# A recurrent attention feeding a mixture of experts: a sum of rows cut into pieces, and two groups of transfers moved to later iterations

## The chip, the core and the metric

The kernel runs on one core of a Trainium2 chip. Its engines work side by side and meet at semaphores: TensorE (PE), VectorE (DVE), ScalarE (ACT), GpSimd (POOL) and SyncE (SP). SP only issues transfers here. Each engine takes its instructions in the order in which they were written, so an instruction that waits holds up everything behind it on that engine. The metric is the device time of one execution in microseconds (us); lower is better.

## What is computed

First a recurrent attention over 4 batches, 8 heads, 768 steps and head width 48, in float32, then a mixture of 8 experts on the 3072 rows that come out of it:

```python
for t in range(S):                                   # attention
    cur = np.einsum('bhd,bhe->bhde', u[None] * kt, vt)
    y[:, :, t] = np.einsum('bhd,bhde->bhe', rt, state + cur)
    state = wt[:, :, :, None] * state + np.einsum('bhd,bhe->bhde', kt, vt)

logits = x @ w_gate + modality_bias[modality_id]     # x: the 3072 rows of 384
e_idx = np.argmax(logits, axis=1)
probs = np.exp(logits - logits.max(-1, keepdims=True))
probs /= probs.sum(-1, keepdims=True) + 1e-09
gate_w = probs[np.arange(N), e_idx]
for e in range(E):                                   # 384 -> 1024 -> 384
    mask = e_idx == e
    h = np.maximum(x[mask] @ w1[e], 0.0)
    out[mask] = gate_w[mask, None] * (h @ w2[e])
```

## The kernel before

**The attention.** The 768 steps of a batch are cut into 6 chunks of 128, so there are 24 units of 128 rows, numbered over all batches. A software pipeline of 26 iterations (`for i in range(-2, NU)`, L970) calls `att_iter(i)`, which works on three units at once: `a = i + 2`, `m = i + 1` and `z = i`. In one iteration

- DVE makes for unit `a` a scan of decays backwards (L413), the scaled keys K (L343, called at L417), a reciprocal and a copy W (L418, L419), a scan forwards and the scaled rows R (`rows_op`, L371), and for unit `m` the masked product A (L462). Between the first scan and the keys it adds two parts of the output of unit `z - 1`, `pY` from TensorE and `dV` from ACT and POOL, into its row buffer `xb` (`x_rows`, L540, calling `x_add`, L537). For units 10 to 13 (`far`) ACT and POOL do that sum.
- POOL makes products for unit `a + 1`: the decays `pw` (L307), `G` (L311) and, in place, the inputs of the next keys and rows (L324). Without these DVE's scan, keys and rows of the next iteration can't start.
- TensorE makes transposes of keys and of sums, the scores `pS` (L460), the state update `pU` (L483), the output `pY` (L503, L514) and the logits (L568). `pS` and `pY` have one buffer each: the next is written when DVE has read the last.

**What SP issues, in order.** At the end of iteration `i`: one of four stores that clear 512 dummy rows of the DRAM buffer `xs` (`fill`, iterations 2 to 5), one of sixteen 192 KB pieces of the first expert's weights (`w_raw` into `raw`, iterations 6 to 21), three loads of r, k and w for unit `i + 6` (until iteration 17) and one load of v for unit `i + 3`. `behind` makes a transfer wait for an instruction of DVE in that iteration: fills and weights for the first scan, v for the masked product.

**The scatters.** The first units are sorted by expert early: in iterations 15 to 20 (`DRAIN`) POOL ends each iteration with one indirect store that scatters 128 finished rows into `xs` (`scatter`, L771). The scatters among themselves write different rows, which `rows_apart` declares, so none waits for another. The fills are declared nothing: a fill and a scatter are two stores into the same DRAM buffer, and the framework orders them as they were written.

**The handover.** After the scatter of iteration 20, `blk_load(0)` (L794; `LOAD = 20`) reads the first block of 512 rows back from `xs` into `xq`. DVE transposes it (L819), ACT and DVE split it into two parts `xh` and `xo` (L827, L829), and TensorE starts the first expert (`blk_up`, L843). From there on 7 blocks are worked off by TensorE, with weights split in two by ACT, DVE and POOL (`w_split`).

Of the kernel before, what the change touches and what calls it, by code (L numbers as in the profile page):

```python
# [14 lines left out]
ALU = mybir.AluOpType  # L15
# [3 lines left out]
P = 128  # L19
NCH = S // P  # L20
NU = B * NCH
NT = B * S
DM = H * D
E, F = 8, 1024
KC = DM // P
FC = F // P
# [4 lines left out]
BW = 512  # L31
# [36 lines left out]
SCATTER = PART[0] + 3  # L68
NEAR = 6
DRAIN = {SCATTER + 2 + n: 1 for n in range(NEAR)}  # L70
EARLY = 6
FILL = 2
APART = 1
NPW = 3
LOAD = SCATTER + 1 + NEAR


@with_exitstack
def kernel(ctx: ExitStack, tc: tile.TileContext, rkw, vt, wf, cst, mid, wg, bias, w1, w2, out):
    nc = tc.nc  # L80
# [20 lines left out]
    ins = [pa.tile([P, WO + WIN], F32, name=f"in{i}", bufs=1) for i in range(NIN)]  # L101
    pw = [pa.tile([P, 4 * SEG], F32, name=f"pw{i}", bufs=1) for i in range(NPW)]
    KT = wk.tile([P, 2, 4, 64], F32, name="KT", bufs=1)
    T = {}

    def wt(n, tag, sh, bufs=None, dt=F32):
        T[tag, n] = (pa if tag in PREP else wk if tag in WORK else rt).tile(sh, dt, tag=tag, name=f"{tag}{n}", bufs=bufs)
        return T[tag, n]
# [7 lines left out]
    def behind(dma, key):  # L116

        if key in step:
            tc.add_manual_dep(dma.ins, step[key].ins.name, mybir.DependencyInfo(mybir.DependencyClass.Sync, mybir.DependencyReason.DATA),
                              reason="transfers of an iteration issued apart")  # L120
# [6 lines left out]
    def r_of(n):  # L127
        return ins[n % NIN][:, RO:RO + 512]
# [4 lines left out]
    def w_of(n):  # L133
        return ins[n % NIN][:, WO:WO + WIN].rearrange("p (a c b) -> p a c b", a=4, c=2)[:, :, :, 0:P // 2]
# [120 lines left out]
    def fill(j):  # L255
        return nc.sync.dma_start(out=xs[DUMMY + j * P:DUMMY + j * P + P, :], in_=zt)
# [36 lines left out]
    def w_raw(e, k, part, cond=None, parts=2):  # L293
        n = FC // parts
        kw = {} if cond is None else {"cond": cond}
        return nc.sync.dma_start(out=raw[k][:, part * n:part * n + n, :].rearrange("p f c -> p (f c)"),
                                 in_=(w1, w2)[k][ds(e, 1), :, part * n * DM:(part + 1) * n * DM].rearrange("a p c -> (a p) c"), **kw)
# [7 lines left out]
    def decays(n, eng):  # L305
        w = w_of(n)
        eng.tensor_tensor(out=heads(pw[n % NPW])[:, :, 2:SEG - 1], in0=w[:, :, 0], in1=w[:, :, 1], op=ALU.mult)  # L307

# [22 lines left out]
    def spread(n, tag, src, c0, bufs=None):  # L331
        X = sides(wt(n, tag, [P, 4, P], bufs).rearrange("p a b -> p (a b)"))
        be, k, v = heads(BE)[:, :, c0:c0 + P // 2], 1 if tag == "K" else 0, sides(src)
        if n == 0:
            w = sides((r_of, k_of)[k](NIN - 1))
            nc.vector.tensor_tensor(out=X[:, :, k], in0=v[:, :, k], in1=be, op=ALU.mult)
            nc.vector.tensor_tensor(out=X[:, :, 1 - k], in0=w[:, :, 1 - k], in1=be, op=ALU.mult)
        elif on_vec(n, k):
            nc.vector.tensor_tensor(out=X[:, :, k], in0=v[:, :, k], in1=be, op=ALU.mult)
            nc.vector.tensor_tensor(out=be, in0=be, in1=w_of(n)[:, :, k], op=ALU.mult)  # L340
            nc.vector.tensor_tensor(out=X[:, :, 1 - k], in0=v[:, :, 1 - k], in1=be, op=ALU.mult)
        else:
            nc.vector.tensor_tensor(out=X, in0=v, in1=be[:, :, None, :].to_broadcast([P, 4, 2, P // 2]), op=ALU.mult)  # L343

    def first(n):
        return n % NCH == 0

    def ok(n):
        return 0 <= n < NU
# [18 lines left out]
    def scan(pp, way):  # L368
        return nc.vector.tensor_tensor_scan(out=BE[:, ::way], data0=pp[:, ::way], data1=d1[:, ::way], initial=0.0, op0=ALU.mult, op1=ALU.max)  # L369

    def rows_op(a):  # L371
        step["second", a - 2] = scan(pw[a % NPW], 1)
        spread(a, "R", r_of(a), 1, 3)

    def dV_tile(z):
# [9 lines left out]
    def att_iter(i):  # L385
        a, m, z = i + 2, i + 1, i
# [11 lines left out]
        if ok(z):  # L398
            if z < NU - 1:
                dV_tile(z)  # L400
            dV, v0, dT = dV_parts(z)
# [6 lines left out]
        if ok(a):  # L408
            t, W = ins[a % NIN], wt(a, "W", [P, 4], 2)
            if a == 0:  # L410
                decays(a, nc.vector)
            pp, n = pw[a % NPW], 4 * SEG
            step["first", i] = scan(pp, -1)  # L413
        if ok(z - 1) and not far(z - 1):
            x_rows(z - 1)
        if ok(a):
            spread(a, "K", k_of(a), 3)  # L417
            nc.vector.reciprocal(out=pp[:, 1:n:SEG], in_=BE[:, 2:n:SEG])  # L418
            nc.vector.tensor_copy(out=W, in_=BE[:, 2:n:SEG])  # L419
        if i == NU - 1:  # L420
            blk_turn(0, (2,))
        if ok(a) and i != -1:
# [54 lines left out]
        if ok(m) and not last:  # L477
# [3 lines left out]
            for h in range(H):  # L481
                p, hh = divmod(h, 2)
# [27 lines left out]
        if ok(z):  # L510
            for h in range(H):
                p, hh = divmod(h, 2)
# [21 lines left out]
    def far(n):  # L534
        return PART[0] <= n <= SCATTER

    def x_add(n, eng, y):  # L537
        eng.tensor_tensor(out=T["xb", n][:, 0:DM], in0=y, in1=T["dV", n].rearrange("p a b -> p (a b)"), op=ALU.add)

    def x_rows(n, eng=None):  # L540
        c = int(n >= PART[0])
        if n in FROM:
            T["xp", c] = (xa, rt)[c].tile([P, PART[c], XW], F32, tag="xp", name=f"xp{c}", bufs=1)
        T["xb", n] = T["xp", c][:, n - FROM[c]]
        y = T["pY", n][:, 0:DM]
        if eng is None:
            x_add(n, nc.vector, y)
        else:
            eng.copy(out=T["xb", n][:, 0:DM], in_=y)

# [417 lines left out]
        pend.extend(range(FROM[c], FROM[c] + PART[c]))  # L968

    for i in range(-2, NU):  # L970
        if EARLY <= i < EARLY + 2 * FC:
            if i == EARLY:
                e0 = nc.sync.value_load(e0i[0:1, 0:1], min_val=0, max_val=E - 1)
        if 1 <= i < 1 + len(SETUP):
            hooks.append(SETUP[i - 1])
        if i == PART[0] + 1:
            ra, tb = route_a(0), table(0)
            hooks.extend([lambda: next(ra), lambda: [*ra], lambda: hook_b(0), lambda: [*tb]])
        if i == NU - 1:
            prep.close()  # L980
        att_iter(i)
        if FILL <= i < FILL + BW // P:
            behind(fill(i - FILL), ("first", i))
        if EARLY <= i < EARLY + 2 * FC:
            behind(w_raw(e0, (i - EARLY) // FC, (i - EARLY + 2) % FC, parts=FC), ("first", i))
        apart = i >= APART
        if i >= -1 and ok(i + 3) and not apart:
            loadv(i + 3)
        if i == -2:
            load(3)  # L990
        if i == 0:
            early()
        if ok(i + 2 + NIN):
            load(i + 2 + NIN, ((512, 1024),))
            load(i + 2 + NIN, ((1024, LIN),), ("second", i) if apart else None)
        if ok(i + 2 + NIN):
            load(i + 2 + NIN, ((0, 512),))
        if ok(i + 3) and apart:
            loadv(i + 3, ("mask", i))
        drain(DRAIN.get(i, 0))  # L1000
        if i == LOAD:
            blk_load(0)
# [28 lines left out]

    part = lambda fn, *a, **k: (lambda: fn(*a, **k))
    q0, q1 = seq[0:2]
    x_rows(NU - 1)
    at(q0, "u", 1, lambda: x_cols(NU - 2, pt(("x", 0), "pX")), lambda: x_cols(NU - 1, pt(("x", 1), "pU")))
    at(q0, "u", 3, part(logits, NU - 2), part(logits, NU - 1))
    for g in range(FC):
# [264 lines left out]
```

## Time and profile before

| what | value |
|---|---|
| median of 3 runs | 331.17 us (330.54 to 331.27) |
| profiled execution, own time | 331.58 us |
| its span, first to last instruction | 329.7 us |
| PE busy | 321.0 us, 97% |
| DVE busy | 237.4 us, 72% |
| ACT busy | 206.3 us, 63% |
| POOL busy | 149.6 us, 45% |
| granted TensorE clock, mean | 0.997 |

All rows below are from the profiled execution. Busy shares are means over the span and hide two stages: the attention up to about 119 us, and the blocks of the experts after it. A PE that shows busy may still run behind another engine, since its matmuls are pipelined and their ends are modelled; starts of instructions say more than busy shares.

### The profile page before, as it was taken

What the parts mean: (1) busy time and instruction counts of PE and PEld (TensorE: products, weight loads), DVE (VectorE), ACT (ScalarE), POOL (GpSimd) and SP (SyncE); (2) the same over time, 40 slices, a digit from 0 to 9 for tenths busy, and PEclk for the clock granted to TensorE, in tenths of its full rate; (3) what the DMA queues carried; (4) which work ended last, traced back from release to release, by engine and by line L of the source; (5) the groups of instructions that cost most, each with busy time, mean ns of one, the idle gap of its engine ahead of it and who ended that gap; (6) DMA issues with size and microseconds to landing.
All of it is one profiled execution on the core that took longest, in us unless ns stands there. A gap on an engine that the chain in (4) does not pass through costs nothing. (4 is left out here: it accounts for less than half of the span.)

```text
span 329.7 us, 10271 instructions
## 1 busy us (share of the span) xinstructions
PE 321.0 (97%) x3917; PEld 297.5 (90%) x3917; DVE 237.4 (72%) x509; ACT 206.3 (63%) x516; POOL 149.6 (45%) x196
## 2 busy tenths in 40 slices
PE   8999999999999999999999999999999999999993
PEld 3789899999998988899889999999999988999983
DVE  7999999999999875795559758858358445815520
ACT  1687587688889894471459456956956944614420
POOL 6889998889886088145861210210210220121022
PEclk9999999999999999999999999999999999999998
DMA  7988988888895601615954800540550673310011
GB/s 260 401 285 254 287 268 268 259 265 261 278 294 163 146 7 55 138 73 188 306 180 123 256 32 2 119 168 2 121 190 4 167 174 97 95 73 22 0 34 55
DMA packets 39023, 52.50 MB, mean 159 GB/s; under 512 B 19221, under 2 KB 26165, under 8 KB 38964
## 3 DMA queue, kind: packets, MB, share of 16 engines
q1 hardware_dynamic: 35860, 42.28, 43.7%
q0 software_dynamic: 3104, 9.47, 7.7%
q8 instruction: 33, 0.54, 0.7%
q14 instruction: 26, 0.21, 0.3%
HBM read 55.63 MB, written 11.88 MB: 205 GB/s over the span
## 5 line engine op out<-in xcount | busy, mean ns | idle before, releaser
L886 POOL DMA_INDIRECT out<-ot,xg x24 | 26.3, 1095 | 128.4 <-ACT ot L885 126.3
L848 DVE SCALAR_TENSOR_TENSOR hl<-pS_u,hh 128x512 fp32r<-128x512 f32 (+2 forms) x56 | 34.6, 618 | 60.7 <-ACT hh L847 60.6
L843 PE MATMUL pS_u<-xh,wh 128*128 128x512 f32 (+2 forms) x168 | 61.1, 364 | 0.0
L843 PE MATMUL pS_u<-xh,wl 128*128 128x512 f32 (+2 forms) x168 | 60.8, 362 | 0.0
L847 ACT ACTIVATE hh<-pS_u 128x512 fp32r<-128x512 f32 (+2 forms) x56 | 30.3, 541 | 48.5 <-PE pS_u L843 48.5
L302 DVE TENSOR_TENSOR wl<-raw,wh 128x768 fp32r<-128x768 f32 x52 | 48.8, 962 | 2.3 <-ACT wh L301 2.0
L301 ACT CAST wh<-raw 128x768 fp32r<-128x768 f32 (+1 forms) x60 | 44.9, 786 | 0.0
L843 PE MATMUL pS_u<-xo,wh 128*128 128x512 f32 (+2 forms) x168 | 42.8, 363 | 0.0
L773 POOL DMA_INDIRECT xs<-xp,posT x24 | 26.3, 1097 | 21.3 <-DVE posT L656 18.1
L369 DVE TENSOR_TENSOR_SCAN pX_s<-pw,pX_s 128x268 f32<-128x268 f32 x48 | 34.3, 715 | 1.2 <-POOL pw L307 0.3
L864 PE MATMUL pY_d<-wh,hh 128*128 128x384 f32 x104 | 35.1, 337 | 0.0
L864 PE MATMUL pY_d<-wh,hl 128*128 128x384 f32 x104 | 35.0, 336 | 0.0
L864 PE MATMUL pY_d<-wl,hh 128*128 128x384 f32 x104 | 34.9, 336 | 0.0
L843 PEld LDWEIGHTS pS_u<-xh,wh 128*128 128x128 f32 x168 | 31.6, 188 | 3.1
L843 PEld LDWEIGHTS pS_u<-xh,wl 128*128 128x128 f32 x168 | 31.6, 188 | 2.8
L843 PEld LDWEIGHTS pS_u<-xo,wh 128*128 128x128 f32 x168 | 30.9, 188 | 3.3 <-DVE xo L829 0.3
L390 ACT ACTIVATE dV<-v,dT 128x48 f32<-128x48 f32 x120 | 29.7, 328 | 0.2 <-POOL pw L307 0.2
L462 DVE TENSOR_TENSOR A<-pS,cs 128x1024 f32<-128x1024 f32 x24 | 29.2, 1218 | 0.6 <-PE pS L460 0.6
L311 POOL TENSOR_TENSOR G<-in 128x512 f32<-128x512 f32 x24 | 26.1, 1090 | 3.6 <-PE pR_x L355 2.5
L460 PE MATMUL pS<-R,K 64*128 64x128 f32 x384 | 27.3, 281 | 0.0
L864 PE MATMUL pX_d<-wh,hh 128*128 128x384 f32 x80 | 27.0, 337 | 0.0
L864 PE MATMUL pX_d<-wh,hl 128*128 128x384 f32 x80 | 26.9, 336 | 0.0
(331 smaller groups left out, 676.1 us busy)
## 6 DMA issues: line engine op xcount, KB each, us to landing
raw<-w SPq DMA_DIRECT2D x24, 768.0 KB
in<-rkw SPq DMA_DIRECT2D x46, 256.0 KB
in<-rkw SPq DMA_DIRECT2D x22, 264.0 KB
v<-vt SPq DMA_DIRECT2D x24, 192.0 KB
wg<-wf SPq DMA_DIRECT2D x8, 576.0 KB
raw<-w SPq DMA_DIRECT2D x16, 192.0 KB
xs<-zt SPq DMA_DIRECT2D x12, 193.0 KB
xq<-xs SPq DMA_DIRECT2D x12, 192.0 KB
```

Source lines behind the costliest of these rows:

```text
L301: nc.scalar.copy(out=wh[k][:, sl], in_=raw[k][:, sl])
L302: (eng or (nc.vector, nc.gpsimd)[k]).tensor_tensor(out=wl[k][:, sl], in0=raw[k][:, sl], in1=wh[k][:, sl].bitcast(F32), op=ALU.subtract)
L369: return nc.vector.tensor_tensor_scan(out=BE[:, ::way], data0=pp[:, ::way], data1=d1[:, ::way], initial=0.0, op0=ALU.mult, op1=ALU.max)
L390: nc.scalar.activation(out=dV[:, h], in_=v0[:, h], func=AF.Copy, scale=dT[:, h:h + 1])
L460: nc.tensor.matmul(out=pS[:, hh, p], lhsT=K[q, p], rhs=R[q, p], start=True, stop=True)
L462: step["mask", i] = nc.vector.tensor_tensor(out=a2(A), in0=a2(pS), in1=mask[:, None, :].to_broadcast([P, H, P]), op=ALU.mult)
L773: rows_apart("xs", nc.gpsimd.indirect_dma_start(out=xs[:, :], out_offset=bass.IndirectOffsetOnAxis(ap=posT[:, n:n + 1], axis=0), in_=T["xb ...
L843: nc.tensor.matmul(out=pp, lhsT=wsrc[0][:, g, c * P:(c + 1) * P], rhs=xsrc[:, c, 0:w], start=(n == 0), stop=(n == 3 * KC - 1))
L847: nc.scalar.activation(out=hh, in_=pp, func=AF.Relu)
L848: nc.vector.scalar_tensor_tensor(out=hl, in0=pp, scalar=0.0, in1=hh.bitcast(F32), op0=ALU.max, op1=ALU.subtract)
L864: nc.tensor.matmul(out=X["y", q, j][0:r1 - r0], lhsT=hsrc[:, r0:r1], rhs=wsrc[1][:, f], start=(f == 0 and n == 0), stop=(f == FC - 1 and n ...
L886: ins = nc.gpsimd.indirect_dma_start(out=out[:, :], out_offset=bass.IndirectOffsetOnAxis(ap=xg[0:m, j, 1:2].bitcast(I32), axis=0), in_=ot[ ...
```

## The change

Three edits.

1. The sum of a unit's rows on DVE is cut into three pieces of 128 columns, put after the first scan, after the copy W and after the second scan. Where unit `a` is the first of a batch there are two pieces, of 256 and 128 columns, after the first scan and after W. In the last two iterations, which have no unit `a`, the sum stays whole.
2. The four fills move from iterations 2 to 5 to iterations 18, 18, 19 and 19.
3. The sixteen pieces of weights start in iteration 10 instead of 6; from iteration 20 on there are two in each iteration, until 22.

```diff
-EARLY = 6
-FILL = 2
+EARLY = (*range(10, 20), 20, 20, 21, 21, 22, 22)
+FILL = (18, 18, 19, 19)
+XCUTS = tuple((c, c + P) for c in range(0, DM, P))
+XLAST = ((0, 2 * P), (2 * P, DM))
...
     def rows_op(a):
         step["second", a - 2] = scan(pw[a % NPW], 1)
+        x_third(2)
         spread(a, "R", r_of(a), 1, 3)
...
         if ok(z - 1) and not far(z - 1):
-            x_rows(z - 1)
+            thirds.extend(x_rows(z - 1, cuts=((XCUTS, XLAST)[first(a)] if ok(a) else ((0, DM),))))
+        x_third(0)
         if ok(a):
             spread(a, "K", k_of(a), 3)
             nc.vector.reciprocal(out=pp[:, 1:n:SEG], in_=BE[:, 2:n:SEG])
             nc.vector.tensor_copy(out=W, in_=BE[:, 2:n:SEG])
+            x_third(1)
...
+    def x_third(k):
+        if thirds:
+            x_add(*thirds.pop(0))
...
-        if FILL <= i < FILL + BW // P:
-            behind(fill(i - FILL), ("first", i))
-        if EARLY <= i < EARLY + 2 * FC:
-            behind(w_raw(e0, (i - EARLY) // FC, (i - EARLY + 2) % FC, parts=FC), ("first", i))
+        for n, at in enumerate(FILL):
+            if i == at:
+                behind(fill(n), ("first", i))
+        for n, at in enumerate(EARLY):
+            if i == at:
+                behind(w_raw(e0, n // FC, (n + 2) % FC, parts=FC), ("first", i))
```

DVE in iteration 5 before, from the first scan to the masked product. `xp` is the row buffer that `xb` points into, `pX_s` holds the scans, and what stands in brackets are the semaphores that an instruction waits for (DVE_49 is DVE's own):

```order
L369 SCALAR_TENSOR_TENSOR pX_s<-pw_93,pX_s 128x268 [waits DVE_49,Pool_49]
L538 TENSOR_TENSOR xp_389<-pY_769,dV_722 128x384 [waits PE_49,Activation_49,Pool_49]
L343 TENSOR_TENSOR K_818<-in_91,pX_s 128x512 [waits DMAHW3_49,DVE_49,Pool_49]
L418 RECIPROCAL pw_93<-pX_s 128x4
L419 COPY W_815<-pX_s 128x4
L369 SCALAR_TENSOR_TENSOR pX_s<-pw_93,pX_s 128x268 [waits DVE_49]
L343 TENSOR_TENSOR R_823<-in_91,pX_s 128x512 [waits DMAHW5_49,DVE_49]
L462 TENSOR_TENSOR A_843<-pS_844,cs 128x1024 [waits PE_49]
```

The same iteration of the change:

```order
L371 SCALAR_TENSOR_TENSOR pX_s<-pw_93,pX_s 128x268 [waits DVE_49,Pool_49]
L543 TENSOR_TENSOR xp_389<-pY_774,dV_726 128x128 [waits PE_49,Activation_49]
L345 TENSOR_TENSOR K_822<-in_91,pX_s 128x512 [waits DMAHW3_49,DVE_49,Pool_49]
L422 RECIPROCAL pw_93<-pX_s 128x4
L423 COPY W_819<-pX_s 128x4
L543 TENSOR_TENSOR xp_389<-pY_774,dV_726 128x128 [waits Activation_49]
L371 SCALAR_TENSOR_TENSOR pX_s<-pw_93,pX_s 128x268 [waits DVE_49]
L543 TENSOR_TENSOR xp_389<-pY_774,dV_726 128x128
L345 TENSOR_TENSOR R_829<-in_91,pX_s 128x512 [waits DMAHW5_49,DVE_49]
L467 TENSOR_TENSOR A_849<-pS_850,cs 128x1024 [waits PE_49]
```

Each of the three instructions that wait for DVE itself (K, the second scan, R) now has a piece of the sum ahead of it.

SP at the end of iterations 17 to 20 before. `raw` are weights, `v` a unit's values; DMAHW semaphores are those of SP's own transfers:

```order
L137 DMA v_2248<-vt 128x384 [waits DMAHW6_49,DVE_49,Activation_49]
L296 ISA
L296 DMA raw_67<-w 128x384 [waits DMAHW7_49,DVE_49]
L137 DMA v_2353<-vt 128x384 [waits DMAHW0_49,DVE_49,Activation_49]
L296 ISA
L296 DMA raw_67<-w 128x384 [waits DMAHW1_49,DVE_49]
L137 DMA v_2466<-vt 128x384 [waits DMAHW2_49,DVE_49,Activation_49]
L296 ISA
L296 DMA raw_67<-w 128x384 [waits DMAHW3_49,DVE_49]
L137 DMA v_2579<-vt 128x384 [waits DMAHW4_49,DVE_49,Activation_49]
```

SP at the end of iterations 17 to 19 of the change. `xs<-zt` is a fill, and DMASW semaphores are those of POOL's scatters:

```order
L139 DMA v_2263<-vt 128x384 [waits DMAHW6_49,DVE_49,Activation_49]
L258 DMA xs<-zt 128x386 [waits DMAHW7_49,DMASW2_49,DVE_49]
L258 DMA xs<-zt 128x386 [waits DMAHW0_49]
L298 ISA
L298 DMA raw_67<-w 128x384 [waits DMAHW1_49]
L139 DMA v_2372<-vt 128x384 [waits DMAHW2_49,DVE_49,Activation_49]
L258 DMA xs<-zt 128x386 [waits DMAHW3_49,DMASW3_49,DVE_49]
L258 DMA xs<-zt 128x386 [waits DMAHW4_49]
L298 ISA
L298 DMA raw_67<-w 128x384 [waits DMAHW5_49]
L139 DMA v_2489<-vt 128x384 [waits DMAHW6_49,DVE_49,Activation_49]
```

The first pair of fills waits for the third scatter (DMASW2, iteration 17), the second pair for the fourth (DMASW3, iteration 18).

POOL before, from the fourth scatter (iteration 18) to the sixth (iteration 20):

```order
L773 DMA xs<-xp_389,posT 29184x386
L307 TENSOR_TENSOR pw_93<-in_90 128x4x64 [waits DMAHW7_49,DVE_49]
L311 TENSOR_TENSOR G_2359<-in_90 128x512 [waits DMAHW6_49,DMAHW0_49,PE_49]
L324 TENSOR_TENSOR in_90<-in_90 128x2x4x64 [waits Pool_49]
L773 DMA xs<-xp_389,posT 29184x386
L307 TENSOR_TENSOR pw_94<-in_91 128x4x64 [waits DMAHW4_49,DVE_49]
L311 TENSOR_TENSOR G_2472<-in_91 128x512 [waits DMAHW5_49,DMAHW3_49,PE_49]
L324 TENSOR_TENSOR in_91<-in_91 128x2x4x64 [waits Pool_49]
L773 DMA xs<-xp_389,posT 29184x386
```

The same stretch of POOL in the change:

```order
L784 DMA xs<-xp_389,posT 29184x386 [waits DMAHW7_49,DMAHW0_49]
L309 TENSOR_TENSOR pw_93<-in_90 128x4x64 [waits DVE_49]
L313 TENSOR_TENSOR G_2378<-in_90 128x512 [waits DMAHW6_49,PE_49]
L326 TENSOR_TENSOR in_90<-in_90 128x2x4x64 [waits Pool_49]
L784 DMA xs<-xp_389,posT 29184x386 [waits DMAHW4_49,DMAHW3_49]
L309 TENSOR_TENSOR pw_94<-in_91 128x4x64 [waits DVE_49]
L313 TENSOR_TENSOR G_2495<-in_91 128x512 [waits DMAHW5_49,PE_49]
L326 TENSOR_TENSOR in_91<-in_91 128x2x4x64 [waits Pool_49]
L784 DMA xs<-xp_389,posT 29184x386
```

The fourth scatter now waits for the first pair of fills (DMAHW7, DMAHW0) and the fifth for the second pair (DMAHW4, DMAHW3); the sixth waits for none, but stands behind the products of unit 23, which stand behind the fifth.

## Rows read from the trace of the kernel before

**Rows 1.** Windows: busy us per engine, clock, DMA share; attention, then blocks.

```profile
20.00:110.00 90.00, 88.01 (x2272) 83.30 (x2267) 87.49 (x170) 72.42 (x266) 75.51 (x108) 1.00 0.82 256
120.00:320.00 200.00, 200.00 (x1119) 188.68 (x1118) 124.65 (x287) 114.91 (x193) 51.66 (x48) 1.00 0.37 108
```

**Rows 2.** Timeline of DVE (start, us, instruction), iterations 12 and 16.

```profile
67.23 0.71 DVE L369 TENSOR_TENSOR_SCAN pX_s<-pw,pX_s 128x268 f32<-128x268 f32 x1
68.03 0.69 DVE L343 TENSOR_TENSOR K<-in,pX_s 128x512 f32<-128x512 f32 x1
...
85.94 0.71 DVE L369 TENSOR_TENSOR_SCAN pX_s<-pw,pX_s 128x268 f32<-128x268 f32 x1
86.56 0.54 DVE L538 TENSOR_TENSOR xp<-pY,dV 128x384 f32<-128x384 f32 x1
87.01 0.68 DVE L343 TENSOR_TENSOR K<-in,pX_s 128x512 f32<-128x512 f32 x1
...
87.70 0.13 DVE L419 COPY W<-pX_s 128x4 f32<-128x4 f32 x1
87.86 0.72 DVE L369 TENSOR_TENSOR_SCAN pX_s<-pw,pX_s 128x268 f32<-128x268 f32 x1
88.62 0.69 DVE L343 TENSOR_TENSOR R<-in,pX_s 128x512 f32<-128x512 f32 x1
```

**Rows 3.** Groups by line and shape, DVE, 15 to 113 us: busy, mean ns, idle before.

```profile
L538 DVE TENSOR_TENSOR xp<-pY,dV 128x384 f32<-128x384 f32 x17 | 9.3, 546 | 0.5 <-POOL pw L307 0.3
```

**Rows 4.** Timeline of DVE, iteration 6: a sum that starts late.

```profile
40.21 0.56 DVE L538 TENSOR_TENSOR xp<-pY,dV 128x384 f32<-128x384 f32 x1 [0.26 <-POOL pw L307]
```

**Rows 5.** Timeline of POOL: third scatter, then the fifth to the sixth.

```profile
90.53 1.01 POOL L773 DMA_INDIRECT xs<-xp,posT  x1 [0.15 <-issue]
...
99.29 1.01 POOL L773 DMA_INDIRECT xs<-xp,posT  x1 [0.15 <-issue]
100.33 0.65 POOL L307 TENSOR_TENSOR pw<-in 128x256 f32<-128x256 f32 x1
101.36 1.09 POOL L311 TENSOR_TENSOR G<-in 128x512 f32<-128x512 f32 x1 [0.37 <-PE pR_x L355]
102.53 1.10 POOL L324 TENSOR_TENSOR in<-in 128x512 f32<-128x512 f32 x1
103.78 1.01 POOL L773 DMA_INDIRECT xs<-xp,posT  x1 [0.15 <-DVE A L462]
```

**Rows 6.** Scatters, issue to landing: third to sixth; 126 to 132 us; all 24.

```profile
DMA to landing us min/median/max: 5.5/5.6/5.8
DMA to landing us min/median/max: 2.7/2.9/3.2
DMA to landing us min/median/max: 2.7/4.2/7.3
```

**Rows 7.** Timeline of SP's issues and DVE: the first load and its first reader.

```profile
0.71 2.29 SPq L125 DMA_DIRECT2D in<-rkw  x5
3.48 0.42 DVE L307 TENSOR_TENSOR pw<-in 128x256 f32<-128x256 f32 x1 [0.64 <-DMA in<-rkw]
```

**Rows 8.** Timelines of SP, DVE, ACT, PE: the first block's handover.

```profile
109.39 1.97 SPq L800 DMA_DIRECT2D xq<-xs  x4
116.40 0.71 DVE L819 STREAM_TRANSPOSE xt<-xq 128x512 f32<-128x512 f32 x1 [0.60 <-DMA xq<-xs]
117.82 0.62 ACT L827 CAST xh<-xt 128x512 fp32r<-128x512 f32 x1
119.41 0.50 PE L843 MATMUL pS_u<-xh,wh 128*128 128x512 f32 x1
```

**Rows 9.** Timeline of DVE, iteration 21: first scan of unit 23.

```profile
108.04 0.71 DVE L369 TENSOR_TENSOR_SCAN pX_s<-pw,pX_s 128x268 f32<-128x268 f32 x1
```

**Rows 10.** Windows at the end, columns as in rows 1: PE stops, then the clock.

```profile
324.00:326.00 2.00, 0.40 (x3) 0.08 (x1) 0.00 (x0) 0.58 (x1) 0.36 (x1) 1.00 0.05 14
326.00:328.00 2.00, 0.00 (x0) 0.00 (x0) 0.00 (x0) 0.00 (x0) 0.62 (x1) 0.88 0.26 98
```

More of the change, by code (lines that the diff above doesn't have):

```diff
@@ L535, in far, with x_add, x_rows @@
         return PART[0] <= n <= SCATTER
-    def x_add(n, eng, y):
-        eng.tensor_tensor(out=T["xb", n][:, 0:DM], in0=y, in1=T["dV", n].rearrange("p a b -> p (a b)"), op=ALU.add)
-    def x_rows(n, eng=None):
+    def x_add(n, eng, y, c0=0, c1=DM):
+        eng.tensor_tensor(out=T["xb", n][:, c0:c1], in0=y[:, c0:c1], in1=T["dV", n].rearrange("p a b -> p (a b)")[:, c0:c1], op=ALU.add)
+    thirds = []
+    def x_third(k):
+        if thirds:
+            x_add(*thirds.pop(0))
+    def x_rows(n, eng=None, cuts=((0, DM),)):
         c = int(n >= PART[0])
@@ L546, in x_rows @@
         if eng is None:
-            x_add(n, nc.vector, y)
+            return [(n, nc.vector, y, *c) for c in cuts]
         else:
@@ L970 @@
     for i in range(-2, NU):
-        if EARLY <= i < EARLY + 2 * FC:
-            if i == EARLY:
+        if i in EARLY:
+            if i == EARLY[0]:
                 e0 = nc.sync.value_load(e0i[0:1, 0:1], min_val=0, max_val=E - 1)
@@ L981 @@
         att_iter(i)
-        if FILL <= i < FILL + BW // P:
-            behind(fill(i - FILL), ("first", i))
-        if EARLY <= i < EARLY + 2 * FC:
-            behind(w_raw(e0, (i - EARLY) // FC, (i - EARLY + 2) % FC, parts=FC), ("first", i))
+        for n, at in enumerate(FILL):
[4 more added lines that the diff above has]
+                behind(w_raw(e0, n // FC, (n + 2) % FC, parts=FC), ("first", i))
         apart = i >= APART
@@ L1033 @@
     q0, q1 = seq[0:2]
-    x_rows(NU - 1)
+    x_add(*x_rows(NU - 1)[0])
     at(q0, "u", 1, lambda: x_cols(NU - 2, pt(("x", 0), "pX")), lambda: x_cols(NU - 1, pt(("x", 1), "pU")))
```

## The prediction

> **What bounds the kernel now.** I read the windows first, then DVE's timeline of the attention, then the timelines of POOL and SP around the handover to the first block. The windows [rows 1] show two stages. In the attention (20 to 110 us) DVE is busy 87.5 of 90 us and PE 88.0, so the two are close; in the blocks (120 to 320 us) PE is busy 200.0 of 200 us at a granted clock of 1.00, and nothing else is full. So a microsecond by which the first block starts later or earlier is a microsecond of the whole: after it there is no gap on PE that could swallow one.
>
> When does the first block start? PE's first L843 is at 119.41 [rows 8]. Backwards from there: SP issues the reads of the block at 109.39, DVE's transposes start at 116.40, having sat idle 0.60 us for them, so the reads take 7.0 us; the first xh is cast from 117.82 to 118.44. PE comes to it only at 119.41, when the attention's last products are done. So two chains end within 1.0 us of each other: the attention itself, and the block's reads with 119.41 - 118.44 = 1.0 us to spare. And the reads hang on the sixth scatter: it starts at 103.78 [rows 5] and lands 5.5 us later (the smallest of the third to sixth, [rows 6]), at 109.28, just ahead of 109.39.
>
> **The change part by part: the pieces.** In iteration 16 the scan starts at 85.94, the whole sum at 86.56, K at 87.01 [rows 2]: 1.07 us from scan to K. In iteration 12, where DVE has no sum, K starts 0.80 us after the scan (67.23 to 68.03). The sum of 0.54 us thus costs only 0.27 us today. The rows say why: K reads the scan and waits 0.09 us beyond its end, while the sum, which doesn't read it, starts 0.09 us before its end. A piece of 128 columns is 256 columns shorter than the sum of 546 ns [rows 3]; 128 more columns cost about 142 ns (R, with 512, takes 0.69 [rows 2]), so the piece takes about 0.27 us, and its slot, less the overlap of 0.09, is about 0.18 us.
> - First piece: starts 0.62 after the scan, frees DVE at 0.80, just when K could start anyway. K moves from 1.07 to 0.81: -0.26 us.
> - Second piece: today the second scan starts 0.16 us after W does (87.70 to 87.86), waiting for DVE's own results. With a piece between, 0.07 (W's 0.13 less the overlap) and 0.18 make 0.25: +0.09.
> - Third piece: R starts 0.76 us after the second scan (87.86 to 88.62), and will at 0.62 + 0.18 = 0.80 or a little more: +0.06.
>
> Together about -0.10 us in an iteration with three pieces. The two pieces of iterations 4, 10 and 16 give -0.13 and +0.09, so -0.04. Three pieces stand in iterations 1 to 9 but 4, in 15, and in 17 to 21: 14 of them; the sum is 14 x 0.10 + 3 x 0.04 = 1.5 us off DVE, 1.0 of it before the third scatter. Not all of that reaches the end, since PE is nearly as full: in iteration 6 the sum starts 0.26 us late [rows 4] although DVE was free, and such waits remain. I take 0.6 us up to the third scatter and 0.9 up to the end of the attention, with bounds of 0 and 1.5. PE can't write the next `pY` before the last piece is read; the third piece ends about 2.7 us into an iteration of 4.4 (from the scan of iteration 16 at 85.94 to that of iteration 21 at 108.04 [rows 2, 9] are five), and PE writes the next `pY` late in its own iteration, so I cost that at nothing; if the cover is gone, it is one or two tenths in a few iterations, within the bounds.
>
> Against this edit speaks a rule of the Trainium skill, "VectorE: DVE Perf Modes", section "Rules for kernel authors": chained instructions pay the flush of the pipeline each time, whether they wait on semaphores or not, so one should cut their number. The trace disagrees here: an instruction that waits for the scan starts 0.09 us after its end, and one that doesn't starts 0.09 us before it [rows 2]. What full payment would cost is a rival below.
>
> **Weights later.** The pieces of weights move, none is added. w1's eight pieces come in iterations 10 to 17, and are first used at the handover; w2's last four pieces are issued after the block's reads, where before there was one. They stand behind the reads on SP's queue and are wanted only when the block's first products are done, so I cost them at nothing. That early iterations have fewer transfers gains nothing that I can see: DVE's idle time before the sum, 0.5 us in 17 of them, is put down to POOL and not to a load [rows 3]. Bounds: a few tenths either way.
>
> **The fills.** This is the edit that decides. Before, all four were landed long before the first scatter. Now they lie between the scatters, and the order of stores into `xs` makes a chain: third scatter lands, first pair of fills is issued and lands, fourth scatter, lands, second pair, lands, fifth scatter. The sixth scatter waits for none, but it is behind unit 23's products on POOL, which are behind the fifth scatter. Then come the block's reads. In numbers:
> - The third scatter starts at 90.53 [rows 5] less 0.6, so 89.9, and lands 5.5 us later [rows 6]: 95.4. SP issues the first pair at 95.5.
> - A pair of fills: the trace has no landing of a fill. The nearest row is the first load, 264 KB, read 3.48 - 0.71 = 2.8 us after its issue [rows 7]; the second fill is issued 0.4 us after the first, and I add 0.2 for the loads ahead of them: 3.4 us. Bounds: a quiet scatter of as many bytes lands in 2.7 us of which 1.0 is POOL's own work, so 1.7 + 0.4 = 2.1; a slow one 5.8, so 5.2. First pair landed: 98.9.
> - Fourth scatter: I take the median of all, 4.2 [rows 6], since only one load of v and one of weights are beside it; bounds 2.7 and 5.8. Landed 103.1, second pair issued 103.2.
> - Second pair, with nothing ahead of it: 2.8 + 0.4 = 3.2. Landed 106.4.
> - Fifth scatter to sixth: 103.78 - 99.29 = 4.5 us, less 0.37 in which POOL waited for PE [rows 5]: 4.1. The sixth starts at 110.5.
> - Sixth scatter: by then little else is in flight, as at 126 to 132 us: 3.2 [rows 6]. Landed 113.7, reads issued at 113.8 instead of 109.39: 4.4 us late.
>
> The 1.0 us to spare at the handover goes first, which leaves 3.4 us. It can't be hidden behind other work: ACT's and POOL's splits of w1 stand behind the casts of xh or go on meanwhile, but PE has nothing left. On the way DVE also waits: its scan for unit 23, at 108.04 [rows 9] less 0.9, needs POOL's decays, which start 1.04 us after the fifth scatter, at 107.4, and take 0.65; its keys need the product in place, done at 110.3. That delays the attention's end by about 1 us, to near 119.6, less than the late reads.
>
> By another rule of the skill, "DMA: Bandwidth & Descriptors", section "Anatomy of one DMA — SWDGE (gpsimd) path", a transfer costs about 2.0 us, mostly the receipt of the write, plus its bytes over 436 GB/s. An estimate by that page gives a fill of 193 KB 2.5 us, both pairs 2.9, and the sum would be 0.8 us smaller; no row here shows a fill alone.
>
> Sum: 331.58 (the profiled execution; span 329.7 and 1.9 around it) + 3.4 = 335.0. That execution is 0.4 above the median of the runs, so the forecast is 334.6.
>
> **The rivals.**
> - *The chain hides.* All transfers land as quietly as at 126 to 132 us. Then 89.9 + 4.2 + 2.1 + 2.7 + 2.1 + 4.1 + 2.7 and 0.2 for issues is 108.0: the sixth scatter lands no later than today, the attention's end decides, and its 0.9 us are won: 330.3. It decides where the reads are issued by 109.39 + 1.0 less what the attention wins. For it: landings of 2.7 to 3.2 exist, and SP's queue is emptier after iteration 17. Against it: the third to sixth scatters all took 5.5 to 5.8, in this very place [rows 6].
> - *The chain is long and the clock falls.* Landings stay at 5.5, pairs take 4.0: 89.9 + 5.5 + 4.0 + 5.5 + 4.0 + 4.1 + 5.5 + 0.3 = 118.8, reads 9.4 late, 8.4 after the spare. PE then stands idle for some 6 us, and at the end of the program the granted clock had fallen within 3 us of PE's last work (0.88 as a mean of 326 to 328 [rows 10]; the lower of its levels, 1.2 GHz, is half). What it takes to come back no row shows; up to 2 us lost. 339.6 to 341.6.
> - *The pieces are paid in full.* No cover: three pieces at 0.27 are 0.81 us, against 0.54 for the whole sum, so +0.27 us in an iteration with three and +0.13 in one with two. By the third scatter that is 9 x 0.27 + 3 x 0.13 = 2.8 us instead of -0.6, and with the chain 338.0. Against it are rows 2.
> - *No change.* The chain costs about what the pieces win: 331.2.
>
> **How the numbers follow.** The forecast chain has 0.52, 331.9 to 338; the long chain 0.14; the pieces in full 0.06; the hidden chain 0.20 and no change 0.08. A measurement of this kernel tells 0.2%, some 0.7 us, from no change. That makes slower 0.72, no change 0.07 and faster 0.21 (the edges of the cases shared out). The range that leaves 1 in 10 on either side is 330.2 to 340.5; the forecast's own is 331.9 to 338.
>
> **What would show it.** Right: in the trace after, K starts about 0.8 us after the first scan with a sum between; the third and fourth scatters are followed by fills that land before the fourth and fifth start; the fifth starts near 106 instead of 99.3, the block's reads near 114 instead of 109.39, the first L843 near 123, and from there on PE's timeline is the old one shifted. POOL's idle time before its scatters is then put down to transfers of `xs`. Wrong: the reads issued before 110.5, or the first L843 before 119.4 (the chain hid); more than 0.7 us between a fill's neighbours than the sum of the rows says (landings mis-sized); an iteration of the attention above 4.45 us (the pieces cost); or a gap on PE in the blocks that swallows the delay.

## The result and the profile after: 1.5% slower

| what | before | after |
|---|---|---|
| median, runs side by side | 331.27 us | 336.63 us (335.9 to 336.84) |
| ratio, 95% interval | | 1.0149 [1.0112, 1.0186] |
| profiled execution, own time | 331.58 us | 336.84 us |
| its span | 329.7 us | 335.0 us |
| first matmul of the first block | 119.41 | 124.56 |
| from there to the end of the span | 210.3 us | 210.4 us |

The last two rows give the place: 5.15 of the 5.3 us are lost before the first block's first matmul, and PE swallows none of it afterwards. The forecast was 334.6, so the sign is right and the size is 2.0 us short. The rest of this section follows the steps from the third scatter to that matmul. Code lines have moved: the scatter is now L784, the block's reads L811, the up-matmul (before L843) L854.

Windows of the profile after (busy us and number of instructions of PE, PEld, DVE, ACT, POOL; granted clock; DMA share; GB/s): the two stages as in [rows 1], and the two microseconds each before the first block.

```profile
20.00:110.00 90.00, 87.44 (x2283) 83.25 (x2279) 84.77 (x192) 72.39 (x264) 71.17 (x103) 1.00 0.78 239
120.00:320.00 200.00, 200.00 (x1221) 189.10 (x1222) 127.31 (x290) 118.32 (x205) 53.05 (x49) 1.00 0.38 111
...
112.00:114.00 2.00, 0.02 (x2) 0.00 (x0) 0.86 (x4) 0.33 (x2) 1.83 (x2) 1.00 0.04 12
114.00:116.00 2.00, 0.88 (x12) 0.91 (x14) 2.00 (x5) 1.73 (x6) 1.30 (x3) 0.75 0.26 99
116.00:118.00 2.00, 2.00 (x39) 2.00 (x38) 0.70 (x1) 0.00 (x0) 0.00 (x0) 0.50 0.40 94
118.00:120.00 2.00, 2.00 (x43) 1.79 (x40) 0.83 (x2) 0.48 (x1) 0.00 (x0) 0.90 1.08 243
```

Most of the attention and all of the blocks look as before. From 112 to 115 PE does next to nothing, and then its clock falls: it is at the lower of its two levels (half of full speed) for the whole of 116 to 118 and for parts of the windows on either side.

The timeline of POOL after (start, us, engine, line, operation; in brackets the idle time before it and who ended it), third to sixth scatter:

```profile
90.55 1.01 POOL L784 DMA_INDIRECT xs<-xp,posT  x1 [0.15 <-issue]
...
101.36 1.01 POOL L784 DMA_INDIRECT xs<-xp,posT  x1 [6.77 <-DMA xs<-zt]
...
109.21 1.01 POOL L784 DMA_INDIRECT xs<-xp,posT  x1 [3.94 <-DMA raw<-w]
...
113.26 1.01 POOL L784 DMA_INDIRECT xs<-xp,posT  x1 [0.15 <-issue]
```

SP's issues after: the two pairs of fills and the block's reads.

```profile
96.23 0.83 SPq L258 DMA_DIRECT2D xs<-zt  x2
...
104.55 0.82 SPq L258 DMA_DIRECT2D xs<-zt  x2
...
116.06 1.94 SPq L811 DMA_DIRECT2D xq<-xs  x4
```

From issue to landing after, of the third, the fourth and the sixth scatter:

```profile
DMA to landing us min/median/max: 5.6/5.6/5.6
...
DMA to landing us min/median/max: 3.1/3.1/3.1
...
DMA to landing us min/median/max: 2.8/2.8/2.8
```

The chain is there link by link. Scatter 90.55 + 5.6 = 96.15, fills at 96.23; POOL sits idle 6.77 us for them until 101.36; + 3.1 = 104.46, fills at 104.55; fifth scatter at 109.21; sixth 4.05 later; + 2.8 = 116.06, and in that instant the reads go out, 6.67 later than in [rows 8]. The releaser of the 3.94 us is given as a piece of weights. What the fifth scatter waits for are the two fills' semaphores, DMAHW4 and DMAHW3, as its listing above shows; releasers are inferred, and the weights were issued at 105.58, right behind the fills.

DVE after, iteration 17, which answers to [rows 2], then three rows of iteration 21 and one of the handover; last, the row of before that answers to K in iteration 21:

```profile
90.26 0.71 DVE L371 TENSOR_TENSOR_SCAN pX_s<-pw,pX_s 128x268 f32<-128x268 f32 x1
90.88 0.27 DVE L543 TENSOR_TENSOR xp<-pY,dV 128x128 f32<-128x128 f32 x1
91.07 0.68 DVE L345 TENSOR_TENSOR K<-in,pX_s 128x512 f32<-128x512 f32 x1
...
91.75 0.13 DVE L423 COPY W<-pX_s 128x4 f32<-128x4 f32 x1
91.80 0.28 DVE L543 TENSOR_TENSOR xp<-pY,dV 128x128 f32<-128x128 f32 x1
92.00 0.71 DVE L371 TENSOR_TENSOR_SCAN pX_s<-pw,pX_s 128x268 f32<-128x268 f32 x1
92.62 0.27 DVE L543 TENSOR_TENSOR xp<-pY,dV 128x128 f32<-128x128 f32 x1
92.81 0.67 DVE L345 TENSOR_TENSOR R<-in,pX_s 128x512 f32<-128x512 f32 x1
...
110.93 0.72 DVE L371 TENSOR_TENSOR_SCAN pX_s<-pw,pX_s 128x268 f32<-128x268 f32 x1 [2.07 <-POOL pw L309]
113.14 0.69 DVE L345 TENSOR_TENSOR K<-in,pX_s 128x512 f32<-128x512 f32 x1 [1.31 <-POOL in L326]
114.70 0.27 DVE L543 TENSOR_TENSOR xp<-pY,dV 128x128 f32<-128x128 f32 x1
...
121.77 1.30 DVE L830 STREAM_TRANSPOSE xt<-xq 128x512 f32<-128x512 f32 x2 [0.82 <-DMA xq<-xs]
...
109.23 0.68 DVE L343 TENSOR_TENSOR K<-in,pX_s 128x512 f32<-128x512 f32 x1
```

K starts 0.81 after the scan, the second scan 0.25 after W, R 0.81 after that scan: the slots are those of the forecast. In iteration 21 the scan waits for POOL, K waits for POOL again, so K starts at 113.14 and not at 109.23, and the third piece comes behind both, at 114.70. PE after, the wait for that piece, the attention's end and the first block; last, the attention's end before:

```profile
115.12 1.23 PE L508 MATMUL pY<-SPb,R 128*64 128x96 f32 x12 [3.10 <-DVE xp L543]
...
123.51 1.12 PE L519 MATMUL pK_('y', 23)_2836<-v,A 128*64 128x48 f32 x32
124.56 0.50 PE L854 MATMUL pS_u<-xh,wh 128*128 128x512 f32 x1
...
118.37 1.12 PE L514 MATMUL pK_('y', 23)_2805<-v,A 128*64 128x48 f32 x32
```

The first block's matmul has no idle time before it. PE came straight from the attention's last product, so in this execution the attention's end decided and not the reads. How much earlier would the reads have let the block start? The casts don't tell. ACT, one row of before, then two of after:

```profile
117.45 0.48 ACT L452 COPY xT<-pS_x 128x384 f32<-128x384 f32 x1
...
122.59 0.48 ACT L457 COPY xT<-pS_x 128x384 f32<-128x384 f32 x1
122.97 1.82 ACT L838 CAST xh<-xt 128x512 fp32r<-128x512 f32 x3
```

In both kernels the casts come, with no idle time, right behind a copy that ACT makes for the attention, so they too hang on the attention. Where PE does wait for the casts and these for DVE's transposes (e2, e6 and e7 below), the block starts 1.4 us after the transposes. By that the reads alone would have allowed 117.8 before (116.40 [rows 8] + 1.4) and 123.2 after (121.77 + 1.4).

### The profile page after: what moved, and what is told of

It reads as the page before. It is cut to its first block, busy times and chain, and to the rows that moved or that the text cites. A ratio compares the mean times of both kernels' runs of the same rounds, so it can differ in the third digit from the quotient of the medians.

```text
span 335.0 us, 10312 instructions
## 1 busy us (share of the span) xinstructions
PE 321.8 (96%) x3917; PEld 298.7 (89%) x3917; DVE 236.4 (71%) x540; ACT 206.7 (62%) x516; POOL 148.9 (44%) x196
## 5 line engine op out<-in xcount | busy, mean ns | idle before, releaser
L854 PE MATMUL pS_u<-xh,wh 128*128 128x512 f32 (+2 forms) x168 | 61.1, 364 | 0.0
L854 PE MATMUL pS_u<-xh,wl 128*128 128x512 f32 (+2 forms) x168 | 60.8, 362 | 0.0
L854 PE MATMUL pS_u<-xo,wh 128*128 128x512 f32 (+2 forms) x168 | 42.9, 363 | 0.0
L784 POOL DMA_INDIRECT xs<-xp,posT x24 | 26.3, 1097 | 31.7 <-DVE posT L667 18.1
L854 PEld LDWEIGHTS pS_u<-xh,wh 128*128 128x128 f32 x168 | 31.6, 188 | 3.1
L854 PEld LDWEIGHTS pS_u<-xh,wl 128*128 128x128 f32 x168 | 31.6, 188 | 2.8
L854 PEld LDWEIGHTS pS_u<-xo,wh 128*128 128x128 f32 x168 | 30.9, 188 | 3.4 <-DVE xo L840 0.4
```

Of the source, the lines that this page charges most:

```text
L784: rows_apart("xs", nc.gpsimd.indirect_dma_start(out=xs[:, :], out_offset=bass.IndirectOffsetOnAxis(ap=posT[:, n:n + 1], axis=0), in_=T["xb ...
L854: nc.tensor.matmul(out=pp, lhsT=wsrc[0][:, g, c * P:(c + 1) * P], rhs=xsrc[:, c, 0:w], start=(n == 0), stop=(n == 3 * KC - 1))
```

## The experiments

All were timed side by side with the kernel before; a median is compared only by the ratio in its line, since chips differ (the kernel before has medians of 331.2 to 333.0 us on them). The main theory is that the loss comes from the chain of stores, from their order and not from their bytes; the rivals put it on the pieces, on the later weights, or on the transfers' own traffic. Starts and waits are read from one execution of each kernel.

| run | edit | median us | ratio, 95% interval |
|---|---|---|---|
| e1_fills_back | the change, fills in 2 to 5 | 332.39 | 1.0038 [1.0009, 1.0067] |
| e2_fills_late_alone | fills alone | 336.80 | 1.0152 [1.0119, 1.0185] |
| e3_pieces_alone | pieces alone | 332.33 | 1.0022 [1.0000, 1.0045] |
| e4_weights_late_alone | weights alone | 331.12 | 0.9998 [0.9968, 1.0027] |
| e5_fills_unordered | the change, no order of fills and scatters | 331.39 | 1.0008 [0.9982, 1.0034] |
| e6_whole_sum_21 | the change, whole sum in iteration 21 | 337.65 | 1.0193 [1.0143, 1.0244] |
| e7_one_link | the change, all fills in iteration 18 | 337.20 | 1.0177 [1.0141, 1.0213] |
| e8_unordered_whole | e5 with whole sums | 330.59 | 0.9967 [0.9939, 0.9994] |
| e9_two_pieces | e1 with two pieces everywhere | 333.84 | 1.0024 [0.9995, 1.0052] |
| e10_unordered_two | e5 with two pieces everywhere | 331.75 | 0.9971 [0.9944, 0.9999] |

**The fills put back (e1).**

```diff
-FILL = (18, 18, 19, 19)
+FILL = (2, 3, 4, 5)
```

> The change with the four fills back in iterations 2 to 5; the pieces and the later weights stay. Chain theory (the order of stores between fills and scatters made the loss): no faster than 330.0 and no slower than 331.2, about 330.4, since the pieces' 0.9 us are left; the fifth scatter near 99 us again and the block's reads near 109. Rival, the pieces are what costs: it stays above 334. Rival, the weights' new places cost: above 332.

1.0038: nearly all of the loss goes with the fills. The time is above the 331.2 that was allowed for: what is left, 0.4%, belongs to the pieces or the weights (e3 and e4 below tell which), and no gain is left.

**The fills alone (e2).** The kernel before with `FILL = (18, 18, 19, 19)`; sums whole, weights early.

> The kernel before with the fills alone moved to iterations 18, 18, 19, 19 (sum whole, weights early). Chain theory: the reads are issued some 6.5 us late, less the 1.0 to spare, so 336.5 to 337.5; the sum in iteration 21 is whole and ahead of the keys, so PE's wait of 3.1 us for it goes, but the reads then decide. Rival, pieces or weights cost: within 1 us of 331.3.

1.0152, the whole loss without any piece. Its timelines of POOL, DVE and PE (this execution took 338.87 us, 2.1 above the median):

```profile
101.91 1.01 POOL L784 DMA_INDIRECT xs<-xp,posT  x1 [8.33 <-DMA xs<-zt]
...
124.36 1.31 DVE L830 STREAM_TRANSPOSE xt<-xq 128x512 f32<-128x512 f32 x2 [4.06 <-DMA xq<-xs]
...
117.87 1.16 PE L465 MATMUL pS<-R,K 64*128 64x128 f32 x16 [2.35 <-DVE A L467]
...
125.78 0.50 PE L854 MATMUL pS_u<-xh,wh 128*128 128x512 f32 x1 [0.21 <-ACT xh L838]
```

and its window of 120 to 122:

```profile
120.00:122.00 2.00, 2.00 (x38) 2.00 (x36) 0.30 (x1) 2.00 (x7) 1.20 (x2) 0.50 1.10 220
```

Here DVE waits 4.06 us for the reads and PE for ACT's cast, as the prediction drew it, but PE only 0.21 us: the attention ends almost as late as the reads. With the sum whole, PE still stood idle 2.35 us in iteration 21, for the masked product A that stands behind POOL's late products, and its clock fell to the lower level as in the change. So neither the pause nor the fall needs the pieces.

**The pieces alone (e3)**, `FILL` and `EARLY` as before, and **the weights alone (e4)**, `FILL` as before and the sum whole.

> The kernel before with the pieces alone. My working: 0.9 us faster (0 to 1.5), 330.4; an iteration with three pieces 4.28 to 4.32 us from scan to scan where DVE is not kept waiting, against 4.42. Rival, each piece paid in full: 4.5 us slower, 335.8.

> The kernel before with the later weights alone: whole sum, fills in iterations 2 to 5. My working: nothing, 330.9 to 331.7. Rival, fewer transfers early let the attention run freer: some 0.9 us faster, since the sums of iterations 6 to 9 then no longer start late. Rival, w2's last pieces come too late behind the block's reads: the first block's products wait, above 332.

The weights cost nothing, 0.9998. The pieces gain nothing, where 0.9 us were expected: 1.0022 with an interval that begins at 1.0000, and with the weights moved too (e1) it lies above 1. If anything they cost some 0.2% to 0.4%.

**The same transfers without their order (e5).** The fills are put into a group of their own, and fills and scatters are declared to write other rows; the block's reads still wait for both.

```diff
...
+        if filled and key == "xs" and first is not False:
+            tc.declare_no_dep(ins.ins, group="fl", reason="dummy rows")
...
-                behind(fill(n), ("first", i))
+                f = fill(n)
+                tc.declare_no_dep(f.ins, group="xs", reason="dummy rows")
+                tc.add_to_no_dep_group("fl", f.ins)
+                filled.append(f)
+                behind(f, ("first", i))
```

> The change with the fills in iterations 18 and 19, but fills and scatters declared to write different rows, so that neither waits for the other; the block's reads still wait for both. The same transfers at the same places. Chain theory: as with the fills back, 330.0 to 331.5; the fourth and fifth scatters near 94.5 and 99 us. Rival, it is the traffic or SP's queue at that place and not the order: it stays near 336.6.

Timelines of POOL and SP of e5 (this execution took 332.91 us, 1.5 above the median; the scatter is L788 here):

```profile
91.06 1.01 POOL L788 DMA_INDIRECT xs<-xp,posT  x1 [0.15 <-issue]
95.26 1.01 POOL L788 DMA_INDIRECT xs<-xp,posT  x1 [0.15 <-issue]
100.84 1.01 POOL L788 DMA_INDIRECT xs<-xp,posT  x1 [0.15 <-issue]
105.01 1.01 POOL L788 DMA_INDIRECT xs<-xp,posT  x1 [0.15 <-issue]
...
95.78 0.83 SPq L258 DMA_DIRECT2D xs<-zt  x2
100.77 0.82 SPq L258 DMA_DIRECT2D xs<-zt  x2
```

This decides between the order and the traffic. The fills are issued in the same iterations and carry the same bytes; the scatters are 4.2 to 5.6 us apart with no wait for them, and the loss is gone (1.0008).

**One link fewer (e7)**, `FILL = (18, 18, 18, 18)`.

> The change with all four fills in iteration 18: one pair of waits (third scatter to fills to fourth scatter) in place of two. Chain theory, from the change's own landings: four fills landed near 102.5, sixth scatter near 110.7, reads near 113.8 instead of 116.06, first block near 122, so 334.0, about half of the loss. Rival, it is the bytes or the place and not the links: unchanged at 336.6.

1.0177 instead of 334.0: a miss. The chain went as expected up to the sixth scatter: the four fills held the fourth scatter until 102.79 (it sat idle 8.49 us), and with the second wait gone the sixth started at 110.90. Then it took 4.0 us to land where 3.1 was allowed for, so the reads went out at 114.90, only 1.2 earlier than in the change, and they took longer: DVE's transposes began 6.9 us behind them (5.7 in the change). In its profiled execution (336.25) the first up-matmul came at 123.20, 1.4 earlier; half of that was lost again: from there to the end of the span it took 211.1 us, and PE, which in the change found the casts done, waited for ACT's, 0.47 us ahead of the block and 0.32 in it. The median was no better than the change's, and the profile doesn't tell why it lies above that execution.

**The sum whole in iteration 21 (e6).** The two-line condition gets `and i != NU - 3`, which takes away the piece that PE waits 3.10 us for.

> The change with the sum whole in iteration 21 alone. In the changed kernel PE waited 3.1 us there for the last piece, and the attention's end set the first block; but the block's reads were ready only 1.0 us earlier. Theory of two chains: 0.9 us faster than the change, 335.7, and then the reads decide. Rival, the wait for the piece is the loss: 3 us faster, 333.6.

1.0193 (337.65 us) instead of 335.7: a miss, and no gain over the change, whose interval overlaps with this one. Windows of e6, in iteration 21 and at the first block:

```profile
114.00:116.00 2.00, 0.17 (x2) 0.17 (x4) 2.00 (x3) 1.55 (x5) 0.47 (x2) 1.00 0.26 99
116.00:118.00 2.00, 2.00 (x46) 1.88 (x48) 1.20 (x2) 0.34 (x3) 0.10 (x1) 1.00 0.85 196
...
124.00:126.00 2.00, 1.84 (x5) 0.95 (x6) 2.00 (x5) 1.56 (x5) 0.00 (x0) 0.72 0.02 4
126.00:128.00 2.00, 2.00 (x6) 1.52 (x6) 1.05 (x2) 2.00 (x7) 1.15 (x2) 0.50 0.00 0
```

Its timelines of PE and DVE there:

```profile
115.83 1.16 PE L465 MATMUL pS<-R,K 64*128 64x128 f32 x16 [2.35 <-DVE A L467]
...
123.86 0.50 PE L854 MATMUL pS_u<-xh,wh 128*128 128x512 f32 x1 [1.92 <-ACT xh L838]
...
122.45 1.30 DVE L830 STREAM_TRANSPOSE xt<-xq 128x512 f32<-128x512 f32 x2 [4.19 <-DMA xq<-xs]
```

The wait of 3.10 us is gone, but not the idle time: PE now waits 0.98 us for the whole sum (111.34) and 2.35 for A, since both stand behind POOL's late products. Its clock did not fall there, so the attention ended earlier, at 121.94, and the first block started at 123.86, 0.7 earlier. But now PE waited 1.92 us for the reads just ahead of the block, and its clock fell at the block's start: from there to the end of the span it took 212.1 us instead of 210.4. In the change the fall lies among the attention's products of iterations 21 and 22.

**Whole sums without the order (e8)**, and **two pieces (e9, e10)**: `cuts=((0, DM),)` in e5, and in e1 and e5 `XLAST` for every unit, so that nothing stands behind the second scan.

> The late fills undeclared to wait for scatters, and the later weights, but the sum whole: the change without its pieces and without the order of stores. If the pieces gain nothing because PE sets the pace of the attention, this is not slower than the same with pieces (331.4): 330.4 to 331.4. If the pieces do gain, it is slower than that by some 0.9 us: 332.3.

> Later weights and fills in iterations 2 to 5, as with the fills put back, but the sum in two pieces everywhere (256 columns after the first scan, 128 after W), none after the second scan. Theory A (pieces cost because the last one stands behind the second scan, so that TensorE waits to write the next output): without the third piece the wait of iteration 1 goes and the time is that of later weights alone, 331.1 (330.8 to 331.6), the first matmul of a block near 118.5. Theory B (any cutting costs, since TensorE sets the pace and more instructions wait on it): about as with three pieces, 332.4. Theory C (the pieces win where DVE sets the pace): 330.4 or less.

> The fills in iterations 18 and 19 declared to touch other rows than the scatters, weights later, the sum in two pieces everywhere. Theory A: as with whole sums and undeclared order taken away, 330.6. Theory B: as with three pieces there, 331.4. Theory C: below 330.2.

e8, 0.9967 [0.9939, 0.9994], is the only one but e10 whose interval lies below 1, and beats both kernels, by 1 us over the one before. Whether PE's wait for the third piece is what the pieces cost stays open. Without a third piece e9 stands at 1.0024, as far up as e3, which speaks for theory B; e10 stands at 0.9971, beside 0.9967 with whole sums (e8) and 1.0008 with three pieces (e5), which speaks for theory A. Three pairs on one chip each (e4 and e8, e9 and e10, e1 and e5) agree that unordered late fills are 0.3% to 0.5% better than early ones, though the two intervals of each pair overlap. The spans of the profiled executions of e4 and e8 are both 328.3, so no profile shows where; that stays open.

## Why the prediction was right, and where not

**No gap in the blocks.** Right: 210.3 and 210.4 us from the first up-matmul to the end.

**The slots of the pieces.** Right on DVE itself: 0.81 for the forecast 0.81, 0.25 for 0.25, 0.81 for 0.80. Scan to scan it is even 4.28 us instead of 4.42 (starts of the masked product in iterations without a wait), 0.14 less where 0.10 was forecast. The Trainium skill, "VectorE: DVE Perf Modes", section "Rules for kernel authors", would have one cut the number of chained instructions; here an iteration with three pieces is the shorter one for DVE, since they fall into gaps in which it waited for its own results.

**"I take 0.6 us up to the third scatter and 0.9 up to the end of the attention."** This step failed: the third scatter starts at 90.55, before 90.53, and without the chain (e1, e3) the attention ends no earlier. The bound 0 was the right value. The masked products of iterations 5 and 12 show it, in e1 and in e4, which has whole sums (DVE's timelines):

```profile
39.75 1.22 DVE L467 TENSOR_TENSOR A<-pS,cs 128x1024 f32<-128x1024 f32 x1
...
71.08 1.22 DVE L467 TENSOR_TENSOR A<-pS,cs 128x1024 f32<-128x1024 f32 x1
```

```profile
37.92 1.22 DVE L467 TENSOR_TENSOR A<-pS,cs 128x1024 f32<-128x1024 f32 x1
...
69.08 1.22 DVE L467 TENSOR_TENSOR A<-pS,cs 128x1024 f32<-128x1024 f32 x1
```

Seven iterations take 31.33 us with pieces and 31.16 without. DVE runs at 4.28 in iterations 6 to 8, and 10 and 11 then take 4.67 and 4.58 where e4 has 4.41 and 4.21: in e1 DVE waits 0.20 us for `pY` in the one and 0.46 ahead of K in the other, where the profile names nothing that it waits for. The waits of the whole attention stand in the groups of DVE after, 15 to 113 us, which answer to [rows 3]:

```profile
L543 DVE TENSOR_TENSOR xp<-pY,dV 128x256 f32<-128x256 f32 x3 | 1.3, 418 | 0.4 <-POOL pw L309 0.2 <-PE pY L519 0.2
...
L543 DVE TENSOR_TENSOR xp<-pY,dV 128x128 f32<-128x128 f32 x43 | 11.9, 277 | 1.5 <-PE pY L519 1.1 <-ACT pU L491 0.5
```

Idle time before the sum was 0.5 us, most of it for POOL; before the pieces it is 1.9, of which 1.3 for PE's `pY` and 0.5 for ACT's `pU`. But 1.07 of the 1.3 is a single wait, at 27.54, behind a stop of PE (see the next step). So DVE is earlier and then waits for others; that PE, with its 88.0 of 90 us, sets the pace fits, but the waits don't show it and no run isolates it.

**"PE can't write the next pY before the last piece is read ... I cost that at nothing."** Wrong in three iterations of the change. PE waits 0.42 us for the third piece early on (at 19.75; 19.68 in e1, 20.08 in e3), 0.38 in iteration 15 (at 84.40; 0.39 in e1, 0.38 in e5), and 3.10 in iteration 21. The first two make 0.8 us, where the prediction had one or two tenths in a few iterations as its bound. Early on, in the change and in e1, PE stops another 0.7 to 0.9 us soon after, for nothing that the profile shows, and DVE then waits 1.07 or 1.25 for `pY`. Such stops stand at other places in the kernel before too (0.7 us in one), so they can't be charged to the pieces.

**The weights.** Right, nothing (e4).

**The fills.** The mechanism is shown by e5 against the change: take the order away and the loss goes (and by e2: the fills alone bring all of it). The sizes of its terms were off in both directions (landings and starts from the fences above):

| step | forecast | measured |
|---|---|---|
| third scatter starts | 89.9 | 90.55 |
| lands | 5.5 | 5.6 |
| first pair, issue to fourth scatter | 3.4 | 5.13 |
| fourth scatter lands | 4.2 | 3.1 |
| second pair, issue to fifth scatter | 3.2 | 4.66 |
| fifth to sixth scatter | 4.1 | 4.05 |
| sixth lands | 3.2 | 2.8 |
| reads issued | 113.8 | 116.06 |

The mis-sized term is the pair of fills, 3.2 us short over both (1.73 + 1.46), near its upper bound of 5.2; the landings gave 1.5 back. By the Trainium skill, "DMA: Bandwidth & Descriptors", section "Anatomy of one DMA — SWDGE (gpsimd) path", an estimate for a pair was 2.9 us; the rows do not agree, with 5.1 and 4.7. (That section is on transfers that GpSimd issues, and the fills are SP's; nor were they alone.) The prediction had priced the loads ahead of the first pair at 0.2 and those behind a pair at nothing; in the change a piece of weights and a v were issued behind the first pair, and three pieces and two v behind the second. Whether they made the pairs long no run isolates.

**"That delays the attention's end by about 1 us, to near 119.6, less than the late reads."** This step failed in its size. The scan and the keys of unit 23 did wait for POOL, as foreseen. The keys were forecast at 110.3 and began at 113.14; the difference of 2.8 is that of the fifth scatter, 109.21 instead of 106.4, and so comes mostly from the pairs. That is 3.9 us later than before (109.23). From there to the attention's last group of products it took another 1.2 us longer (113.14 to 123.51, before 109.23 to 118.37), which the forecast had not priced. PE stood still for 3.1 us there and its clock fell: the 32 products of L519 in that stretch took 1.92 us, at full clock 1.1. The third piece, which frees `pY` for PE and stood behind both waits, moved the pause but isn't what made it: with the whole sum the same stretch took 10.1 us in e2, where the clock fell too, and 8.5 in e6, where it did not (in the change 10.4).

**"... the block's reads with 119.41 - 118.44 = 1.0 us to spare."** The reading was wrong: the cast that ends at 118.44 hangs on the attention as well, and the reads had some 1.6 us to spare (117.8 against 119.41). Nor did the reads keep their 7.0 us; in the change DVE's transposes began 5.7 us behind them (116.06 to 121.77).

**The sum.** Forecast: reads 4.4 us late, less 1.0 to spare, 3.4. Measured: reads 6.67 late, less 1.3 by which they were shorter, less 1.6 to spare, 3.8; and the attention 1.4 later than that, 5.15. So the chain is the cause, and most of the loss would stand by the reads alone, but in this execution the attention decided, which the forecast excluded. It was close: the reads took 6.7 to 7.2 us in e2, e6 and e7, and with that both chains would end within 0.4 us of each other. The forecast came as near as it did partly by luck, since errors of both signs met: the pairs, the pieces and the attention made the time longer than forecast, the landings, the shorter reads and the larger spare made it shorter.

**The rivals.** The hidden chain needed reads before 110.5 and is out, and no change is out. Pieces paid in full are out by DVE's rows. The long chain with a falling clock was nearest in kind: the clock did fall, but in the change behind a pause within the attention that POOL's late products made, not behind one for the reads (as it did in e6); and its price of 339.6 was too high, since the landings did not stay at 5.5.

## What to carry to other kernels

A store that is moved between other stores into the same DRAM buffer takes its place in their order: count the links of write, landing and issue that this makes, and declare rows apart where they are apart. When two engines are both nearly full, a shorter iteration on one of them may be worth nothing, as here (4.28 us instead of 4.42 on DVE, and a ratio of 1.0022): look first for what the other engines will make it wait for. What is put behind a waiting instruction waits with it, on its own engine and on the engines that need it; taking one such piece away (e6) did not help here, since the next instruction stood behind the same wait. A spare between two chains has to be read from an instruction that hangs on only one of them.

## What the hardware showed that was not expected

- A pause of PE of the same length has not always the same price. In iteration 21 PE stood idle 2.35 us for A in e2 and in e6, with 0.13 and 0.17 us of work in the window of 2 us. In e6 it went on at a granted clock of 1.00; in e2 the clock was 0.86 and 0.50 in the next two windows, the second wholly at the lower level. Later in e6 a pause of 1.92 us ahead of the first block was followed by 0.72 and 0.50. No run here shows what tells them apart.
- The same two fills of 193 KB each took very different times, from the first one's issue to the scatter that waited for them: 5.1, 7.4 and 4.9 us for the first pair and 4.7, 4.0 and 5.4 for the second (the change, e2, e6), while scatters in the change landed in 2.8 to 5.6.
- Four fills in one iteration held the fourth scatter by 8.49 us of idle time (e7). Two held it 6.77 in the change, 6.15 in e6 and 8.33 in e2, so from single executions no price of the other two can be read.
